# Gathered expert rows turned by moves within SBUF and VectorE blocks instead of TensorE transposes

## The chip, the cores and the metric

One core of a Trainium2 chip runs the whole program in one launch. The metric is the device time of one execution in microseconds. Five engines work beside each other, each through its own instructions in order: TensorE (PE), VectorE (DVE), ScalarE (ACT), GpSimd (POOL) and SyncE (SP, which here only issues DMAs). SBUF is the working memory with 128 partitions, PSUM holds matmul results in eight banks of 512 float32 a partition.

## The reference, cut to what matters

Attention with a window and sink tokens gives x of 1536 tokens by 512; a dense layer pair follows, `(h - tanh(h)) @ w_out` with `h = x @ w_in`. Then comes the part that the change touches, a mixture of 8 experts of which each token uses two:

```
logits = x @ w_gate + log1p(exp(x @ w_noise)) * noise
top2, top2_w = the two largest of each row, softmax of the two
for e in range(8):
    for k in range(2):
        mask = top2[:, k] == e
        h = maximum(x[mask] @ w1[e], 0)
        out[mask] += top2_w[mask, k] * (h @ w2[e])
```

## The kernel before, in words

The routing writes a table in DRAM: for each expert a list of up to 424 slots (296 for list 0, and 160 for a list 8 that holds expert 0's late tokens), each with the row of x, the row of out and the weight. Unused slots point at row 0 and write out of bounds. Tokens beyond a list's slots go to overflow sections, worked by `beyond` at the end in a loop that is entered only if there are any.

The experts run one after another, list by list. A list has eight units `u`. Unit by unit, `b_l1` makes h (128 hidden columns by 424 tokens: twelve matmuls, for the three products of split weights and split x, over four slices of 128 of the 512 inputs), `b_chain` makes hh from h (ACT the relu and upper part, DVE the remainder), and `b_l2` adds hh into four accumulators y (twelve matmuls). h has two PSUM banks, so hh of one unit must be out of its bank before the h two units later writes there. The weights come as 1 MB loads `rawi<-wm` on SP (1 KB of w1 and w2 columns a partition each) into two buffers and are split by ACT (cast) and DVE (remainder) into `wi` and `wo` some units ahead.

Around them each list v has these steps:

- `b_gather(v)` (L861): SP loads the list's table, `tab` (L866 the full tiles of 128, L868 the rest), and POOL starts one indirect gather (L857) for each tile of 128 tokens, here four, the last with 40 rows, into `graw`.
- `b_trans(v, k)` for k = 0 to 3 (L884): PE turns each tile's 128 columns of slice k (L890, `xgp<-ident,graw`), ACT casts the upper part from PSUM (L891), DVE takes the remainder (L892). The result `xg` is x of the list with inputs on partitions and tokens along the row.
- `b_prev(v)`: POOL gathers the present rows of out (`prev`).
- `b_evac`, `b_out`, `b_write`: the accumulators are copied out (`yt`, L944), PE turns them back (L972, `yp`), DVE scales and adds `prev` (L957, `y`), POOL scatters to out (L958). The gathers of `prev` wait until the scatters of the list before are in.

In the code `b_gather(e + 1)` comes in unit 1 of list e, `b_trans(e + 1, k)` in unit 4, `b_out(e - 1, m)` in units 0 to 3. The tile framework's scheduler then places every instruction in its engine's row; what an engine waits for is a semaphore, and whatever stands behind a waiting instruction of the same engine waits too.

Of the kernel before, what the change touches and what calls it, by code (L numbers as in the profile page):

```python
# [71 lines left out]
def kernel(ctx: ExitStack, tc: tile.TileContext, qkv, vsink, w64, wm, wgn, noise, out,  # L72
# [48 lines left out]
    def bank(tag, name, w=512):  # L121
        return psp.tile([P, w], F32, tag=tag, name=name, bufs=banks[tag])
# [729 lines left out]
    def tiles(v):  # L852
        w = width(v)
        return [(m, o, min(P, w - o)) for m, o in enumerate(range(0, w, P))]

    def gather(dst, src, t, m, n, rows=NT):
        nc.gpsimd.indirect_dma_start(out=dst, out_offset=None, in_=src[:rows],  # L857
                                     in_offset=bass.IndirectOffsetOnAxis(ap=t[:n, m, 0:1], axis=0),
                                     bounds_check=rows - 1, oob_is_err=False)

    def b_gather(v):  # L861
        t = gp2.tile([P, 4, 4], I32, tag="tab", name=f"tab{v}", bufs=3)
        w = width(v)
        full = w // P
        if full:
            nc.sync.dma_start(t[:, :full], table[v * W:v * W + full * P].rearrange("(m p) w -> p m w", p=P))  # L866
        if w % P:
            nc.sync.dma_start(t[:w % P, full], table[v * W + full * P:v * W + w])  # L868
        tabs[v] = t
        graw[v] = []  # L870
        for m, o, n in tiles(v):
            if m % 2 == 0:
                r = wp.tile([P, 1024], F32, tag="cacz"[m:m + 2], name=f"graw{v}_{m}", bufs=1)
            x = r[:n, (m % 2) * 512:(m % 2) * 512 + 512]
            gather(x, x2d, t, m, n, NT if v else LATE * CT)
            graw[v].append(x)

    def d_bank(name):
        spare["d"].append(spare["d"].pop(0))
        return bank(spare["d"][-1], name)  # L880
# [3 lines left out]
    def b_trans(v, k):  # L884
        w = width(v)
        if v not in xg:
            xg[v] = (yp if v % 2 else gp2).tile([P, 4, 2, W], F32R, tag="xg", name=f"xg{v}", bufs=1)
        pt = bank("as"[k % 2], f"xgp{v}_{k}") if v == 1 and k > 1 else d_bank(f"xgp{v}_{k}")
        for m, o, n in tiles(v):
            nc.tensor.transpose(pt[:, o:o + n], graw[v][m][:, k * P:(k + 1) * P], ident[:n, :n])  # L890
        nc.scalar.copy(xg[v][:, k, 0, :w], pt[:, :w])  # L891
        nc.vector.tensor_sub(xg[v][:, k, 1, :w], pt[:, :w], xg[v][:, k, 0, :w].bitcast(F32))  # L892

# [82 lines left out]
    def c_rows():  # L976
        b_gather(E)
        x = yp.tile([P, 4, WB], F32, tag="xc", name="xc", bufs=1)
        for k in range(4):
            pt = d_bank(f"xcp{k}")  # L980
            for m, o, n in tiles(E):
                nc.tensor.transpose(pt[:, o:o + n], graw[E][m][:, k * P:(k + 1) * P], ident[:n, :n])
            nc.vector.tensor_copy(x[:, k], pt[:, :WB])
        xg[E] = x

# [20 lines left out]
    def beyond(nt):  # L1006

        with ExitStack() as inner:
            op = inner.enter_context(tc.tile_pool(name="op", bufs=1, side="right"))
            tags = {}  # L1010

            def body(row, wrow):
                t = op.tile([P, 1, 4], I32, name="o_tab")
                nc.sync.dma_start(t[:, 0], table[bass.ds(row, P)])
                x = op.tile([P, 512], F32, name="o_x")
                r = op.tile([P, 512], F32, name="o_r")
                gather(x, x2d, t, 0, P)
                gather(r, out, t, 0, P)
                xt = op.tile([P, 512], F32, name="o_xt")
                tp = bank("t", "o_tp")  # L1020
                for k in range(4):
                    nc.tensor.transpose(tp[:, k * P:(k + 1) * P], x[:, k * P:(k + 1) * P], ident)
                nc.vector.tensor_copy(xt, tp)
                yb = bank("a", "o_y")
                for d in range(4):
                    w = op.tile([P, 2048], F32, name="o_w")
                    nc.sync.dma_start(w[:, None], wm[bass.ds(wrow + d, 1)].rearrange("a p n -> p a n"))
                    for s in range(2):
                        h = bank("h", "o_h")
                        for k in range(4):  # L1030
                            nc.tensor.matmul(h[:, :P], w[:, k * 256 + s * P:k * 256 + (s + 1) * P],
                                             xt[:, k * P:(k + 1) * P], start=k == 0, stop=k == 3)
                        g = op.tile([P, P], F32, name="o_g")
                        nc.vector.tensor_scalar(g, h[:, :P], 0.0, None, op0=ALU.max)
                        nc.tensor.matmul(yb, g, w[:, 1024 + s * 512:1536 + s * 512],
                                         start=d == 0 and s == 0, stop=d == 3 and s == 1)
                nc.vector.scalar_tensor_tensor(r, yb, t.bitcast(F32)[:, 0, 2:3], r, op0=ALU.mult, op1=ALU.add)
                nc.gpsimd.indirect_dma_start(out=out[:, :],
                                             out_offset=bass.IndirectOffsetOnAxis(ap=t[:, 0, 1:2], axis=0),
                                             in_=r, in_offset=None, bounds_check=NT - 1, oob_is_err=False)  # L1040

            with tc.For_i(0, E, 1) as e:
                n = nc.values_load(nt[0:1, bass.ds(e, 1)], min_val=0, max_val=OT)
                with tc.For_i(0, n, 1) as i:
                    body(e * SEC + i * P + OV, e * 4)
            n = nc.values_load(nt[0:1, E:E + 1], min_val=0, max_val=OT)
            with tc.For_i(0, n, 1) as i:
                body(i * P + (OV + E * SEC), 0)


    def in_order(k0, k1, engines):

        last = {}
        for i in nc.cur_bb.bb.instructions[k0:k1]:
            if i.engine not in engines:
                continue
            if i.engine in last:
                tc.add_manual_dep(i, last[i.engine],
                                  mybir.DependencyInfo(mybir.DependencyClass.NoSync, mybir.DependencyReason.DATA),
                                  reason="order")  # L1060
            last[i.engine] = i.name
# [146 lines left out]
    while len(routes) > 1:  # L1208
        pull_routes()
    xp_ctx.__exit__(None, None, None)  # L1210
    yp = ctx.enter_context(tc.tile_pool(name="yp", bufs=1, side="right"))
    r5 = routes.pop(0)

    def r(k=1):
# [66 lines left out]
        b_out(E, m)  # L1281
    T = mybir.EngineType
    in_order(marks["a", N1 - 1], marks["a", N1 + 8], (T.PE, T.DVE, T.Activation, T.Pool, T.SP))
    most = nc.values_load(nt[0:1, E + 1:], min_val=0, max_val=OT)
    with tc.If(most > 0):  # L1285
        beyond(nt)
# [54 lines left out]
```

## Time and profile before

| | us |
|---|---|
| three runs | 775.86, 777.5, 781.93 |
| median | 777.5 |
| the profiled execution | 779.83 |
| its span, first to last instruction | 778.1 |
| PE busy | 743.8 |
| DVE busy | 462.1 |
| ACT busy | 356.9 |
| POOL busy | 229.1 |

All times inside the profile count from the start of the span. PE ends list 0 at 452 and list 1 at 500, and then works one list every 41.4 us. "Idle before" in a row is the time in which the engine had nothing running, with what ended it. Issuing a DMA is not counted as busy; `POOL DMA_INDIRECT` rows are the issuing of gathers and scatters, not their transfer.

### The profile page before, as it was taken

What the parts mean: (1) busy time and instruction counts of PE and PEld (TensorE: products, weight loads), DVE (VectorE), ACT (ScalarE), POOL (GpSimd) and SP (SyncE); (2) the same over time, 40 slices, a digit from 0 to 9 for tenths busy, and PEclk for the clock granted to TensorE, in tenths of its full rate; (3) what the DMA queues carried; (4) which work ended last, traced back from release to release, by engine and by line L of the source; (5) the groups of instructions that cost most, each with busy time, mean ns of one, the idle gap of its engine ahead of it and who ended that gap; (6) DMA issues with size and microseconds to landing.
All of it is one profiled execution on the core that took longest, in us unless ns stands there. A gap on an engine that the chain in (4) does not pass through costs nothing. (4 is left out here: it accounts for less than half of the span.)

```text
span 778.1 us, 12237 instructions
## 1 busy us (share of the span) xinstructions
PE 743.8 (96%) x4478; PEld 666.3 (86%) x4479; DVE 462.1 (59%) x1140; ACT 356.9 (46%) x786; POOL 229.1 (29%) x240
## 2 busy tenths in 40 slices
PE   6888999999999999999989989999999999999996
PEld 3565888888999999988888969999999999999996
DVE  5899688778776684445647536455445445544221
ACT  4977688766543352334445424334333333333111
POOL 4444364521000000003064352414233342423223
PEclk9999999999999999999999979999999999999999
DMA  7453121008431140000015265534445453544331
GB/s 261 136 177 107 55 69 43 2 1 290 155 109 55 55 163 1 27 29 28 28 50 178 79 218 199 189 111 151 170 164 179 144 205 133 197 141 130 144 109 66
DMA packets 29697, 92.36 MB, mean 119 GB/s; under 512 B 8365, under 2 KB 11693, under 8 KB 22976
## 3 DMA queue, kind: packets, MB, share of 16 engines
q1 hardware_dynamic: 19232, 63.58, 24.3%
q0 software_dynamic: 8624, 23.75, 9.0%
q10 hardware_dynamic: 1776, 4.19, 1.5%
q8 instruction: 37, 0.61, 0.3%
q14 instruction: 28, 0.23, 0.1%
HBM read 78.65 MB, written 13.58 MB: 119 GB/s over the span
## 5 line engine op out<-in xcount | busy, mean ns | idle before, releaser
L907 PE MATMUL h<-xg,wi 128*128 128x424 f32 (+1 forms) x768 | 161.7, 357 | 0.0
L600 PE MATMUL h<-xT,wi 128*128 128x256 f32 x1152 | 158.6, 284 | 2.0 <-ACT wi L221 2.0
L600 PEld LDWEIGHTS h<-xT,wi 128*128 128x128 f32 x1152 | 150.8, 189 | 9.1 <-ACT wi L221 2.2
L931 PE MATMUL y<-hh,wo 128*128 128x424 f32 (+1 forms) x768 | 152.3, 347 | 0.0
L632 PE MATMUL acc<-wo,g 128*128 128x512 f32 x576 | 151.8, 396 | 0.0
L907 PEld LDWEIGHTS h<-xg,wi 128*128 128x128 f32 x768 | 138.2, 190 | 4.4
L931 PEld LDWEIGHTS y<-hh,wo 128*128 128x128 f32 x768 | 139.5, 188 | 2.5
L632 PEld LDWEIGHTS acc<-wo,g 128*128 128x128 f32 x576 | 101.4, 189 | 16.7
L917 ACT ACTIVATE hh<-h 128x424 fp32r<-128x424 f32 (+1 forms) x64 | 32.5, 510 | 152.3 <-PE h L907 131.2
L918 DVE SCALAR_TENSOR_TENSOR hh<-h,hh 128x424 fp32r<-128x424 f32 (+1 forms) x64 | 37.2, 582 | 89.6 <-ACT hh L917 72.3
L810 POOL DMA_INDIRECT table<-trow,sl x24 | 25.3, 1054 | 217.5 <-DVE sl L807 211.4
L958 POOL DMA_INDIRECT out<-y,tab x33 | 41.1, 1246 | 159.7 <-DVE y L957 159.3
L401 POOL TENSOR_TENSOR e<-e,nm 128x528 f32<-128x528 f32 (+1 forms) x48 | 50.1, 1044 | 79.1 <-DVE nm L399 47.5
L613 ACT CAST g<-th 128x256 fp32r<-128x256 f32 x96 | 38.8, 404 | 61.9 <-PE acc L632 38.6
L610 DVE TENSOR_TENSOR th<-h,th 128x256 f32<-128x256 f32 x96 | 40.4, 420 | 38.3 <-ACT th L608 32.2
L608 ACT ACTIVATE th<-h 128x256 f32<-128x256 f32 x96 | 36.6, 381 | 54.7 <-PE h L600 49.5
L615 DVE TENSOR_TENSOR g<-th,g 128x256 fp32r<-128x256 f32 x96 | 43.2, 450 | 25.2 <-ACT g L613 23.7
L390 ACT ACTIVATE e<-e,nm 128x264 f32<-128x264 f32 (+1 forms) x96 | 47.2, 492 | 23.6 <-DVE nm L377 21.4
L481 PE MATMUL xb<-pT,v 128*128 128x256 f32 x220 | 48.5, 349 | 4.5 <-DVE xT L496 2.4
L857 POOL DMA_INDIRECT prev<-out,tab x33 | 36.8, 1115 | 41.6 <-DMA out<-y,tab 21.9
L227 DVE TENSOR_TENSOR wi<-rawi,wi 128x1024 fp32r<-128x1024 f32 x32 | 39.6, 1236 | 11.5 <-ACT wi L226 8.8
L481 PEld LDWEIGHTS xb<-pT,v 128*128 128x128 f32 x220 | 33.2, 195 | 13.9 <-issue 5.4
(183 smaller groups left out, 949.2 us busy)
## 6 DMA issues: line engine op xcount, KB each, us to landing
rawi<-wm SPq DMA_DIRECT2D x31, 1024.0 KB
rawi<-w SPq DMA_DIRECT2D x8, 1024.0 KB
rawo<-w SPq DMA_DIRECT2D x8, 1024.0 KB
qr<-qkv SPq DMA_DIRECT2D x23, 256.0 KB
rawc<-wm SPq DMA_DIRECT2D x4, 1024.0 KB
out<-zero POOLq DMA_DIRECT2D x1, 3072.0 KB
x2d<-x ACTq DMA_DIRECT2D x6, 512.0 KB
v<-qkv SPq DMA_DIRECT2D x6, 256.0 KB
```

Of the source, the lines that this page charges most:

```text
L227: (nc.gpsimd if (kind, d) in POOL_SPLITS else nc.vector).tensor_sub(t[:, 1], r, t[:, 0].bitcast(F32))
L390: nc.scalar.activation(e[:, h], e[:, h], AF.Exp, bias=nm[:, h, 0:1], scale=-1.0, accum_out=nm[:, h, 2:3])
L401: nc.gpsimd.tensor_mul(e, e, nm[:, :, 3:4].to_broadcast([P, 2, C]))
L481: nc.tensor.matmul(o, l, r_, start=t == 0, stop=t == len(todo) - 1)
L600: nc.tensor.matmul(h[:, :CT], w[:, wa, k * 256 + s * P:k * 256 + (s + 1) * P], x[:, k, xa, ts], start=t == 0, stop=t == 11)
L610: nc.vector.tensor_sub(th, h[:, :CT], th)
L613: nc.scalar.copy(g[:, 0], th)
L615: nc.vector.tensor_sub(g[:, 1], th, g[:, 0].bitcast(F32))
L632: nc.tensor.matmul(acc[c][m], g[:, ga, m * P:(m + 1) * P], w[:, wa, s:s + 512], start=first and t == 0, stop=done and t == 2)
L907: nc.tensor.matmul(h[:, :width(e)], w[:, wa, k * 256 + s * P:k * 256 + (s + 1) * P], xg[e][:, k, xa, :width(e)], start=t == 0, stop=t == 11)
L931: nc.tensor.matmul(yacc[e][m][:, :width(e)], w[:, wa, s + m * P:s + (m + 1) * P], g[:, ga], start=u == 0 and t == 0, stop=u == NU2 - 1 and ...
L958: i = nc.gpsimd.indirect_dma_start(out=out[:, :], out_offset=bass.IndirectOffsetOnAxis(ap=t[:n, m, 1:2], axis=0), in_=y, in_offset=None, b ...
```

## The change

For lists 2 to 7 PE no longer turns the gathered rows. The four gathers write one tile `gr` of 128 x 4 x 512, with 128 rows in the last tile too. Sixteen DMAs on SP (a block of 32 partitions to another, each with 3 or 4 pieces of 128 floats a partition) rearrange it to `rl`: four quarter-rows of a token's 512 values, each on its own 32 partitions, in groups of 32 tokens. Then DVE's transpose turns 32x32 blocks: one instruction of 128 x 448 for each k gives `xt`, with inputs on partitions and tokens along the row. ACT's cast and DVE's remainder read `xt` from SBUF instead of `xgp` from PSUM. Since the inputs are cut in quarters of 128 and eighths of 32 in another order, w1 of experts 2 to 7 is permuted on the host, and the overflow code permutes x likewise for those experts. Lists 0, 1 and 8 keep the PE transposes, with a last tile of 128 rows. The table comes in one load. The pool `yp` is closed ahead of the overflow code, which may use its space.

```
 def b_gather(v):
     t = gp2.tile([P, 4, 4], I32, tag="tab", name=f"tab{v}", bufs=3)
     w = width(v)
-    full = w // P
-    if full:
-        nc.sync.dma_start(t[:, :full], table[v * W:v * W + full * P].rearrange("(m p) w -> p m w", p=P))
-    if w % P:
-        nc.sync.dma_start(t[:w % P, full], table[v * W + full * P:v * W + w])
+    full = (w + P - 1) // P
+    nc.sync.dma_start(t[:, :full], table[v * W:v * W + full * P].rearrange("(m p) w -> p m w", p=P))
     tabs[v] = t
+    if 2 <= v < E:
+        x = yp.tile([P, full, 512], F32, tag="gr", name=f"gr{v}", bufs=1)
+        for m, o, n in tiles(v):
+            gather(x[:, m], x2d, t, m, P)
+        r = yp.tile([P, groups(w), P], F32, tag="rl", name=f"rl{v}", bufs=1)
+        for q in range(4):
+            n = len(range(q, groups(w), 4))
+            for b in range(4):
+                nc.sync.dma_start(r[32 * b:32 * b + 32, q::4], x[32 * q:32 * q + 32, :n, P * b:P * b + P])
+        graw[v] = r
+        return
...
-        x = r[:n, (m % 2) * 512:(m % 2) * 512 + 512]
-        gather(x, x2d, t, m, n, NT if v else LATE * CT)
+        x = r[:, (m % 2) * 512:(m % 2) * 512 + 512]
+        gather(x, x2d, t, m, P, NT if v else LATE * CT)
...
 def b_trans(v, k):
...
+    if v > 1:
+        if k % 2 == 0:
+            xt = wp.tile([P, 2, 32 * groups(w)], F32, tag="cacz"[k:k + 2], name=f"xt{v}_{k}", bufs=1)
+            graw[v, k] = xt[:, 0]
+            graw[v, k + 1] = xt[:, 1]
+        pt = graw.pop((v, k))
+        nc.vector.transpose(pt.rearrange("p (g t) -> p g t", t=32), graw[v][:, :, 32 * k:32 * k + 32])
+        nc.scalar.copy(xg[v][:, k, 0, :w], pt[:, :w])
+        nc.vector.tensor_sub(xg[v][:, k, 1, :w], pt[:, :w], xg[v][:, k, 0, :w].bitcast(F32))
+        return
...
-        nc.tensor.transpose(pt[:, o:o + n], graw[v][m][:, k * P:(k + 1) * P], ident[:n, :n])
+        nc.tensor.transpose(pt[:, o:o + P], graw[v][m][:, k * P:(k + 1) * P], ident)
...
+    w1 = np.concatenate([w1[:2], w1[2:].reshape(E - 2, 4, 4, 32, 1024).swapaxes(1, 2).reshape(E - 2, 512, 1024)])
```

The scheduler places the new steps as follows. On PE the sixteen transposes of each of lists 2 to 7 are gone, and nothing else changes its order. SP, around the table of list 1 (first row) and of list 2 (the next `tab`), before:

```order
L866 DMA tab_5192<-table 128x3x4
L868 DMA tab_5192<-table 40x4
L866 DMA tab_5432<-table 128x3x4
L868 DMA tab_5432<-table 40x4
L1284 TENSOR_LOAD nt
L1284 ISA x2
L182 DMA rawi_5361<-wm 128x2048
L182 DMA rawi_5465<-wm 128x2048
```

The same place after, where `rl_5445` and `gr_5432` are list 2's:

```order
L869 DMA tab_5191<-table 128x4x4
L869 DMA tab_5430<-table 128x4x4
L1316 TENSOR_LOAD nt
L1316 ISA x2
L881 DMA rl_5445<-gr_5432 32x3x128 x2
L881 DMA rl_5445<-gr_5432 32x4x128 x2
L182 DMA rawi_5359<-wm 128x2048
L881 DMA rl_5445<-gr_5432 32x4x128 x6
L881 DMA rl_5445<-gr_5432 32x3x128 x6
L182 DMA rawi_5478<-wm 128x2048
```

The weight load that came right after the tables now stands behind four moves of list 2, and these wait for list 2's four gathers. SP around the table of list 4, before:

```order
L866 DMA tab_6145<-table 128x3x4
L868 DMA tab_6145<-table 40x4
L182 DMA rawi_6178<-wm 128x2048
L182 DMA rawi_6260<-wm 128x2048
L182 DMA rawi_6366<-wm 128x2048
L182 DMA rawi_6435<-wm 128x2048
```

After:

```order
L869 DMA tab_6145<-table 128x4x4
L182 DMA rawi_6193<-wm 128x2048
L881 DMA rl_6160<-gr_6147 32x4x128 x8
L881 DMA rl_6160<-gr_6147 32x3x128 x8
L182 DMA rawi_6275<-wm 128x2048
L182 DMA rawi_6367<-wm 128x2048
L182 DMA rawi_6436<-wm 128x2048
```

One weight load stands ahead of the sixteen moves of list 4 and three behind; lists 5 to 7 have the same order. DVE in units 1 to 3 of list 3, where list 4 is prepared, before (`y_6100` are the output tiles of list 2, `wi` and `wo` the splits):

```order
L918 SCALAR_TENSOR_TENSOR hh_6105<-h_6061,hh_6105 128x424
L957 SCALAR_TENSOR_TENSOR y_6100<-yp_0_6095,tab_5432,prev_5916 128x512
L918 SCALAR_TENSOR_TENSOR hh_6162<-h_6108,hh_6162 128x424
L227 TENSOR_TENSOR wi_6368<-rawi_6260,wi_6368 128x1024
L957 SCALAR_TENSOR_TENSOR y_6100<-yp_1_6136,tab_5432,prev_5916 128x512
L227 TENSOR_TENSOR wo_6335<-rawi_6178,wo_6335 128x1024
L918 SCALAR_TENSOR_TENSOR hh_6204<-h_6165,hh_6204 128x424
```

After:

```order
L942 SCALAR_TENSOR_TENSOR hh_6105<-h_6061,hh_6105 128x424
L981 SCALAR_TENSOR_TENSOR y_6100<-yp_0_6095,tab_5430,prev_5930 128x512
L942 SCALAR_TENSOR_TENSOR hh_6177<-h_6108,hh_6177 128x424
L908 STREAM_TRANSPOSE xt_0_6306<-rl_6160 128x448 x2
L981 SCALAR_TENSOR_TENSOR y_6100<-yp_1_6136,tab_5430,prev_5930 128x512
L908 STREAM_TRANSPOSE xt_2_6313<-rl_6160 128x448
L910 TENSOR_TENSOR xg_6305<-xt_0_6306,xg_6305 128x424 x2
L910 TENSOR_TENSOR xg_6305<-xt_2_6313,xg_6305 128x424
L908 STREAM_TRANSPOSE xt_2_6313<-rl_6160 128x448
L227 TENSOR_TENSOR wo_6336<-rawi_6193,wo_6336 128x1024
L942 SCALAR_TENSOR_TENSOR hh_6219<-h_6180,hh_6219 128x424
```

The four block transposes and three of the remainders now stand between the hh of two neighbouring units in the list's second and third unit; before, the remainders stood in its fifth and sixth, behind PE's transposes, and a weight split stood here in their place.

## Rows read from the trace of the kernel before

**Rows 1.** The page: busy time, and the granted clock in 40 slices.

```profile
PE 743.8 (96%) x4478; PEld 666.3 (86%) x4479; DVE 462.1 (59%) x1140; ACT 356.9 (46%) x786; POOL 229.1 (29%) x240
...
PEclk9999999999999999999999979999999999999999
```

**Rows 2.** Stretches: busy us (instructions) of each engine, granted clock, DMA share, GB/s.

```profile
453.00:457.40 4.40, 0.60 (x2) 0.22 (x2) 0.92 (x2) 0.41 (x1) 2.28 (x3) 0.77 0.90 289
457.40:466.00 8.60, 8.59 (x29) 6.89 (x30) 2.40 (x4) 2.26 (x5) 4.01 (x4) 0.52 0.56 201
...
541.00:582.40 41.40, 41.40 (x226) 39.38 (x226) 20.76 (x27) 15.01 (x22) 14.38 (x12) 1.00 0.49 165
```

**Rows 3.** PE in order of time, list 4's turn: start, length, what.

```profile
575.01 1.33 PE L890 MATMUL xgp<-ident,graw 128*128 128x128 f32 x8
...
582.39 2.48 PE L907 MATMUL h<-xg,wi 128*128 128x424 f32 x12
...
586.99 1.31 PE L907 MATMUL h<-xg,wi 128*128 128x424 f32 x6
```

**Rows 4.** Groups by shape, 430 to 778 us: busy us, mean ns, idle before.

```profile
L890 PE MATMUL xgp<-ident,graw 128*128 128x128 f32 x84 | 15.7, 295 | 0.3 <-DMA graw<-x2d,tab 0.3
...
L890 PE MATMUL xgp<-ident,graw 40*128 40x40 f32 x28 | 7.4, 263 | 3.5 <-DMA graw<-x2d,tab 3.5
```

**Rows 5.** PE in order of time at the turn of list 1.

```profile
453.59 0.33 PE L890 MATMUL xgp<-ident,graw 128*128 128x128 f32 x1 [0.32 <-DMA graw<-x2d,tab]
457.41 3.59 PE L890 MATMUL xgp<-ident,graw 40*128 40x40 f32 x13 [3.50 <-DMA graw<-x2d,tab]
```

**Rows 6.** POOL in order of time, gathers of list 1 and after.

```profile
446.37 1.06 POOL L857 DMA_INDIRECT graw<-x2d,tab  x1 [3.39 <-DMA tab<-table]
...
450.77 1.20 POOL L857 DMA_INDIRECT graw<-x2d,tab  x1 [0.30 <-issue]
...
454.90 0.99 POOL L857 DMA_INDIRECT prev<-out,tab  x1 [0.30 <-issue]
```

**Rows 7.** SP's queue in order of time: tables of list 1, weight loads.

```profile
443.86 0.38 SPq L866 DMA_DIRECT2D tab<-table  x1
444.29 0.41 SPq L868 DMA_DIRECT2D tab<-table  x1
...
451.13 0.34 SPq L182 DMA_DIRECT2D rawi<-wm  x1
...
552.73 0.33 SPq L182 DMA_DIRECT2D rawi<-wm  x1
```

**Rows 8.** POOL in order of time: last scatter to list 4's gathers.

```profile
530.21 1.65 POOL L958 DMA_INDIRECT out<-y,tab  x1 [4.09 <-DVE y L957]
...
542.76 1.66 POOL L857 DMA_INDIRECT graw<-x2d,tab  x1 [0.30 <-issue]
...
547.33 0.98 POOL L857 DMA_INDIRECT graw<-x2d,tab  x1 [0.30 <-issue]
```

**Rows 9.** Stretches, columns as in rows 2, around the end of list 4's gathers.

```profile
547.40:550.10 2.70, 2.70 (x16) 2.65 (x15) 1.43 (x3) 1.99 (x4) 0.92 (x1) 1.00 0.84 334
550.10:552.70 2.60, 2.60 (x15) 2.54 (x14) 2.60 (x3) 1.35 (x2) 0.00 (x0) 1.00 0.02 6
```

**Rows 10.** DVE in order of time, units 2 to 4 of list 3.

```profile
558.31 0.60 DVE L918 SCALAR_TENSOR_TENSOR hh<-h,hh 128x424 fp32r<-128x424 f32 x1 [2.13 <-ACT hh L917]
559.25 1.23 DVE L227 TENSOR_TENSOR wi<-rawi,wi 128x1024 fp32r<-128x1024 f32 x1 [0.34 <-ACT wi L226]
...
570.57 0.75 DVE L957 SCALAR_TENSOR_TENSOR y<-yp,tab,prev 40x512 f32<-40x512 f32 x1
```

**Rows 11.** PE in order of time: three h's, the first and the last.

```profile
560.19 2.57 PE L907 MATMUL h<-xg,wi 128*128 128x424 f32 x12
...
570.28 1.41 PE L907 MATMUL h<-xg,wi 128*128 128x424 f32 x6
```

**Rows 12.** ACT in order of time: the split that follows in list 1.

```profile
471.06 1.04 ACT L226 CAST wi<-rawi 128x1024 fp32r<-128x1024 f32 x1
```

More of the change, by code (lines that the diff above doesn't have):

```diff
@@ L859, in gather, with groups @@
                                      bounds_check=rows - 1, oob_is_err=False)
+    def groups(w):
+        return (w + 31) // 32
     def b_gather(v):
@@ L981, in c_rows @@
             for m, o, n in tiles(E):
-                nc.tensor.transpose(pt[:, o:o + n], graw[E][m][:, k * P:(k + 1) * P], ident[:n, :n])
+                nc.tensor.transpose(pt[:, o:o + P], graw[E][m][:, k * P:(k + 1) * P], ident)
             nc.vector.tensor_copy(x[:, k], pt[:, :WB])
@@ L1010, in beyond, with body @@
             tags = {}
-            def body(row, wrow):
+            def body(row, wrow, turned=False):
                 t = op.tile([P, 1, 4], I32, name="o_tab")
@@ L1019, in body @@
                 xt = op.tile([P, 512], F32, name="o_xt")
+                if turned:
+                    nc.vector.tensor_copy(xt.rearrange("p (k q j) -> p k q j", k=4, q=4),
+                                          x.rearrange("p (q k j) -> p k q j", k=4, q=4))
+                    x = xt
+                    xt = op.tile([P, 512], F32, name="o_xp")
                 tp = bank("t", "o_tp")
@@ L1040, in body @@
                                              in_=r, in_offset=None, bounds_check=NT - 1, oob_is_err=False)
[L1042 to L1045, printed above, removed]
+            for e0, e1 in ((0, 2), (2, E)):
+                with tc.For_i(e0, e1, 1) as e:
+                    n = nc.values_load(nt[0:1, bass.ds(e, 1)], min_val=0, max_val=OT)
+                    with tc.For_i(0, n, 1) as i:
+                        body(e * SEC + i * P + OV, e * 4, e0 > 0)
             n = nc.values_load(nt[0:1, E:E + 1], min_val=0, max_val=OT)
@@ L1210 @@
     xp_ctx.__exit__(None, None, None)
-    yp = ctx.enter_context(tc.tile_pool(name="yp", bufs=1, side="right"))
+    yp_ctx = tc.tile_pool(name="yp", bufs=1, side="right")
+    yp = yp_ctx.__enter__()
     r5 = routes.pop(0)
@@ L1283 @@
     in_order(marks["a", N1 - 1], marks["a", N1 + 8], (T.PE, T.DVE, T.Activation, T.Pool, T.SP))
+    yp_ctx.__exit__(None, None, None)
     most = nc.values_load(nt[0:1, E + 1:], min_val=0, max_val=OT)
```

## The prediction, made before the changed kernel was run

> **What bounds the kernel now.** I read the page first, then the table of stretches for the expert stage, then PE's order of time, then the engines and queues that feed it. The page has PE busy for 743.8 of 778.1 us, with the granted clock down in few slices [rows 1]. The table of stretches says it more sharply: in 541 to 582.4 us, which is one whole list (call it a round of 41.4 us), PE is busy for 41.40 of 41.40 us at full clock, while DVE works 20.76, ACT 15.01, and the DMA engines are used to 0.49 [rows 2]. So in the lists a microsecond of PE is a microsecond of the kernel, and everything else counts only when it makes PE wait. One stretch is different: from 453 to 457.4 us PE does 0.60 us of work while the DMA engines are 0.90 busy, and the 8.6 us after it run at a clock of 0.52, the lower of the two levels [rows 2].
>
> **The transposes that leave PE.** The turn of a list begins on PE at 575.01 and holds sixteen transposes, one unit of twelve h matmuls cut in three, and twelve y matmuls; the next h begins at 582.39. An undisturbed pair of h and y takes 586.99 - 582.39 = 4.60 us [rows 3]. The turn therefore costs 7.38 - 4.60 = 2.78 us. Six lists lose it (of 124 such transposes 96 go): 6 x 2.78 = **-16.7 us**, all on the engine that has no gap.
>
> **Full last tiles.** Lists 0, 1 and 8 keep the transposes on PE, with 128 rows instead of 40 or 32 in the last tile: 12 transposes that go from 263 to 295 ns mean [rows 4], 12 x 0.03 = **+0.4 us** (0 from below, as a shape of one length; 12 x 0.3 = 3.5 from above, if each were a whole transpose more).
>
> **List 1.** PE waits 3.50 us there, until 457.41, for the fourth gather of the list [rows 5]. POOL had issued it at 450.77 and was done with it at 451.97 [rows 6], but SP issued a 1 MB load at 451.13 [rows 7], and the engines then were 0.90 busy. In the changed order this load stands behind the first four moves of list 2, and these wait for list 2's gathers, which POOL cannot begin before its last prev gather is out, at 454.90 + 0.99 = 455.9 [rows 6]. So the fourth gather meets an idle DMA. What that is worth I read from list 4: its fourth gather is issued by 547.33 + 0.98 = 548.3 [rows 8], and the DMA engines fall from 0.84 to 0.02 at 550.1 [rows 9], 1.8 us later. That gives 451.97 + 1.8 = 453.8; 88 more rows at 2.70 us for 424 [rows 9] add 0.6. PE would go on at 454.4: -3.0 us. If the clock then does not fall, 8.6 us at 0.52 become 4.5: another -4.1 us, together -7. Against this stands the load that went back in the queue: four gathers take 547.33 + 0.98 - 542.76, about 5.6 us [rows 8], so they are out at 461.5 and landed at 463.3; four moves take 1.7 us more, and the load leaves at 465 instead of 451. With the 6.3 us that it took before (451.13 to 457.4, when the busy stretch of rows 2 ends) it lands at 471.3. Before, ACT split it at 471.06 [rows 12]. On the old times it is just in time; with PE 7 us earlier it is late, and ACT, which has h's activation behind the split, waits. I give back 3 of the 7 and take **-4 us** (bounds -7, all kept; +3, if the wait outlasts the gain).
>
> **The new chain for lists 2 to 7.** Per list come 16 moves on SP, four DVE transposes of 448 wide, and the split now reads SBUF. Neither the moves nor the block transpose are in this trace. A move: back-to-back issues on SP stand 0.43 us apart [rows 7], and POOL could use the tables at 446.37, 1.7 us after the second issue ended at 444.70 [rows 6, 7]. So 16 x 0.43 + 1.7 = 8.6 us from gather to last landing (from below 16 x 0.34 + 1.7 = 7.1, by the load's own issue time in rows 7; from above 16 x 0.43 + 6.3 = 13.2, if the last one queues behind a 1 MB load). I take 8.6, since the two tables are the nearest kind of transfer. A block transpose: the longest DVE row works 1024 elements in 1.23 us [rows 10], so 448 take 0.54; from above 1.23 whole, from below 0.3 (twice that rate). I take 0.55, because all DVE rows near it are about this dear per element. The split's subtraction I leave at the 0.60 of a 424-wide row [rows 10] (0.5 to 0.7).
>
> The Trainium skill (VectorE: DVE Perf Modes, The three transpose paths and Rules for kernel authors) speaks against the swap: for a 128x128 transpose it says to use TensorE where PSUM will do, and it gives DVE 311 ns for such a block in bf16, so an estimate by that page is 3.5 x 311 = 1.09 us here, with which each round below is 2.2 us longer and the whole about 768. No run here shows that price yet.
>
> DVE takes its work in order, so the transposes hold up what stands behind. In the round of list 4 (times of before, less the 2.78 us of the turn that lies between the last out scatter and here): the hh row ahead of the transposes ends at 558.31 + 0.60 - 2.78 = 556.1 [rows 10]. The gathers are in at 550.1 [rows 9], the moves at 558.7. DVE waits 2.6 us. Behind the transposes come 4 x 0.55 + 0.75 (y) + 3 x 0.60 + 1.22 (split) = 6.0 us until the next hh, which ends at 565.3. That hh frees one of two h banks: the h begun at 560.19 has its bank written again at 570.28 [rows 11], less 2.78 is 567.5. So 2.2 us are left, and PE does not wait. But the chain closes on itself: the last y of the list follows at 565.3 + 0.75 + 0.60 + 1.23 + 0.60 + 0.75 = 569.2 instead of 570.57 + 0.75 - 2.78 = 568.5 [rows 10], and from it hang the out scatter, prev, the next gathers and the next moves: from 530.21 [rows 8] to 558.7 are 28.5 us, plus 10.5 to the last y and 0.3 to its scatter, 39.3 us around. PE's new round is 41.4 - 2.8 = 38.6. Each round falls 0.7 us further back, and the 2.2 us last for about lists 4 to 7. I take **+1 us** (0 to +18; the upper end is below). The weights' loads, which SP now issues behind the moves, are 5 us late (552.73 before [rows 7], about 557.4 in the same times); a split that waits for one comes after the transposes anyway.
>
> **Sum.** -16.7 + 0.4 - 4 + 1 = -19.3. The profiled execution took 779.83 us (778.1 of span and 1.7 around it): 760.5. It is 2.3 above the median of the three runs, 777.5, from which the same sum gives 758.2. I forecast 759.5.
>
> **Rivals.**
> *The chain takes PE's place.* If a move waits behind a load (stage 13.2 us), list 4 loses 4.6 - 2.2 = 2.4 us, and the three rounds after it are 43.9 instead of 38.6, 3 x 5.3 = 15.9: together 18, and 760.5 - 1 + 18 = 778, no change. With block transposes of 1.23 us it is 2.7 more per round: 0.5 + 3 x 3.4 = 10.7, 770. Half way 772. For it speaks that 39.3 stands so near to 38.6; against it that the DMA engines are idle right after the gathers [rows 9].
> *Slower: the moves run one after another.* Each of 16 small transfers then costs up to the 1.7 us from issue to use. With s us from gather to last move, list 4 loses s - 10.8 and each of three further rounds s - 7.9. The gain of 19.3 is used up, and 1% more, when 4s - 34.5 = 27, s = 15.4, that is 0.86 us a move. At 1.0, between 0.43 and 1.7, s is 17.7, the loss 36, and the time 797. For it speaks only that nothing in this trace moves SBUF to SBUF. Against it: SP issued two table loads 0.43 apart and both were usable 1.7 us after the second [rows 6, 7].
> The Trainium skill (SBUF — State Buffer, Summary: rules for kernel authors) is on this rival's side: for a transfer bound by DMA it wants 128 partitions and "one DMA, not several", and here are sixteen on 32 partitions. The trace neither agrees nor disagrees: it has no such set.
> *List 1 alone.* Nothing gained there is 764, all of it 757.5; both lie in the forecast's own range, 751 to 768. That the transposes stay on PE is no rival: the changed order has none for lists 2 to 7.
>
> **How the numbers follow.** Forecast with its own range 0.67; chain in PE's place 0.20; slower 0.13. A measurement of this kernel tells 1% from no change, here 769.7 and 785.3. All of the first case is faster; of the second 0.06 ends under 769.7 and 0.14 over it; the third is slower: 0.73, 0.14, 0.13. The range has to reach the second case, to 779, and from below 751 (all of list 1 kept, no give-back, the median's basis, and some room): about 0.13 above and 0.04 below are left out.
>
> **What would show it.** Right: no transposes in PE's rows for lists 2 to 7; rounds near 38.6 to 39.5 us with PE without a gap; the fourth gather of list 1 in by 455; DVE idle two to three microseconds ahead of the first block transpose of lists 4 to 7; block transposes of 0.5 to 0.6 us; the last move landed under 9 us after the gathers. Wrong: PE gaps ahead of h, with hh late behind a block transpose; block transposes over 1 us; moves further apart than 0.5 us; a clock below 1.00 anywhere in lists 2 to 7; or rounds that stay at 41.4.

## The result and the profile after

The changed kernel takes **789.7 us** (median of 5 runs, 784.9 to 792.1) against 778.3 for the kernel before in the same comparison: a ratio of 1.014, 95% interval 1.009 to 1.019. It is slower by 1.4%; the forecast was 759.5, with a range from 751 to 779. The profiled execution took 784.91 us, 783.2 of them span. Ratios and intervals here are of fast runs alone, and of e11's four runs one was slow (782.5 us), so that its time below is the median of the other three.

The page after, busy time and the granted clock in 40 slices (before: [rows 1]):

```profile
PE 733.0 (94%) x4382; PEld 659.6 (84%) x4383; DVE 468.3 (60%) x1164; ACT 354.8 (45%) x786; POOL 227.4 (29%) x240
...
PEclk9999999999999999999999999989989998999998
```

PE has 96 matmuls fewer and 10.8 us less to do, yet the span is 5.1 us longer. The clock row shows where to look: its one dip of before, at list 1, is gone, and there are three new ones further on in the lists (the fourth 8 is the end of the program, behind the lists). The table of stretches after (columns as in [rows 2]), one list of 40 us and the three dips:

```profile
530.00:570.00 40.00, 37.49 (x198) 35.56 (x197) 14.24 (x19) 11.41 (x17) 13.19 (x10) 1.00 0.50 151
...
514.70:521.50 6.80, 5.58 (x16) 5.29 (x17) 6.34 (x11) 3.11 (x5) 1.12 (x1) 0.50 0.84 340
...
572.70:579.50 6.80, 4.80 (x14) 4.50 (x15) 5.40 (x8) 2.10 (x5) 2.01 (x2) 0.50 0.59 206
...
658.00:664.90 6.90, 5.70 (x16) 5.35 (x17) 4.85 (x8) 2.27 (x5) 2.01 (x2) 0.51 0.54 186
```

Before, PE was busy 41.40 of 41.40 us in such a stretch [rows 2]. Now it has gaps, and after a gap it ran at the lower of the two levels (0.50, 1.2 GHz) for some 6.8 us. Twelve matmuls of h took 4.61 us there and 2.57 at full clock, so the 5.58 + 4.80 + 5.70 = 16.1 us of work done at that level would have taken 9.0: some 7 us are the clock's.

PE after, in order of time, at list 1 and in the round in which list 4 is made ready:

```profile
453.19 1.64 PE L914 MATMUL xgp<-ident,graw 128*128 128x128 f32 x13 [0.31 <-DMA graw<-x2d,tab]
454.59 0.87 PE L931 MATMUL h<-xg,wi 128*128 128x424 f32 x3
...
570.47 0.62 PE L996 MATMUL yp<-ident,yt 128*40 128x128 f32 x4 [2.58 <-DVE y L981]
574.70 4.61 PE L931 MATMUL h<-xg,wi 128*128 128x424 f32 x12 [3.61 <-DVE hh L942]
```

List 1 went as forecast, or better: the fourth gather makes PE wait 0.31 us instead of 3.50 [rows 5], the clock stays up. Later PE waits for y and then for hh, and the next h takes 4.61 us instead of the 2.57 of [rows 11]. The waits after, from 430 us on (what waited for what: us in total, times, longest):

```profile
ACT wi L226 <- DMA rawi<-wm: 63.7, 23, 6.7
ACT xg L909 <- DVE xt L908: 50.0, 14, 12.3
DVE xt L908 <- DMA rl<-gr: 47.5, 6, 12.2
PE h L931 <- DVE hh L942: 13.8, 6, 5.6
...
PE yp L996 <- DVE y L981: 3.6, 2, 2.6
...
SPq L881 <- DMA gr<-x2d,tab: 62.9, 9, 14.3
```

PE's 13.8 + 3.6 us and 0.4 of issue, together 18, and the clock's 7 are the loss of the lists in this trace. Three waits can stand behind them: DVE's for the moves, with ACT's for DVE's transposes behind it; ACT's for weight loads (2.8 us in all in the kernel before); and SP's, at the head of the moves, for the gathers. SP, DVE, ACT and POOL after, in that same round, in order of time:

```profile
543.57 0.33 SPq L182 DMA_DIRECT2D rawi<-wm  x1
556.69 10.23 SPq L881 DMA_DIRECT2D rl<-gr  x16
567.37 7.16 SPq L182 DMA_DIRECT2D rawi<-wm  x2
```

```profile
556.10 0.60 DVE L942 SCALAR_TENSOR_TENSOR hh<-h,hh 128x424 fp32r<-128x424 f32 x1 [1.82 <-ACT hh L941]
568.61 1.17 DVE L908 STREAM_TRANSPOSE xt<-rl 128x448 f32<-128x448 f32 x2 [11.91 <-DMA rl<-gr]
...
574.05 0.59 DVE L942 SCALAR_TENSOR_TENSOR hh<-h,hh 128x424 fp32r<-128x424 f32 x1
```

```profile
569.29 1.07 ACT L909 CAST xg<-xt 128x424 fp32r<-128x424 f32 x2 [10.41 <-DVE xt L908]
...
572.21 1.04 ACT L226 CAST wi<-rawi 128x1024 fp32r<-128x1024 f32 x1 [0.67 <-DMA rawi<-wm]
573.16 0.52 ACT L941 ACTIVATE hh<-h 128x424 fp32r<-128x424 f32 x1
```

```profile
534.38 1.64 POOL L982 DMA_INDIRECT out<-y,tab  x1 [5.94 <-DVE y L981]
...
547.57 1.03 POOL L857 DMA_INDIRECT gr<-x2d,tab  x1 [0.30 <-issue]
```

SP starts no weight load between 543.57 and 567.37; before there was one at 552.73 [rows 7]. DVE stands 11.91 us ahead of the first block transpose, 18 us pass between two hh. And the gathers themselves come late (547.57, where before the first was at 542.76 [rows 8]), because the last scatter of the list ahead came at 534.38: the circle is closed.

What holds hh is read from the rows just ahead of it. ACT stands 10.41 us for the transposes, and only then 0.67 for the load; and what PE waits for at 570.47 is a y that DVE computes right behind its first transposes. At the first and longest gap, 5.59 us ahead of 515.92, where list 3 is made ready, no load comes in at all: hh follows the first block transpose on DVE, and ACT had done its part of it by 503.1.

```profile
514.74 0.65 DVE L908 STREAM_TRANSPOSE xt<-rl 128x448 f32<-128x448 f32 x1 [12.17 <-DMA rl<-gr]
515.31 0.56 DVE L942 SCALAR_TENSOR_TENSOR hh<-h,hh 128x424 fp32r<-128x424 f32 x1
```

DVE's six waits are 1.1, 12.2, 11.9, 5.8, 10.4 and 6.2 us for lists 2 to 7, and PE's three long gaps ahead of h fall on the three above 10. But when ACT then comes to its next split, the load is 0.4 to 0.7 us short of landed in all three, so this trace alone can't say what either wait would cost without the other. The block transposes are nearly as cheap as forecast, 0.63 us (group by line, 430 us to the end):

```profile
L908 DVE STREAM_TRANSPOSE xt<-rl 128x448 f32<-128x448 f32 x24 | 14.6, 629 | 47.5 <-DMA rl<-gr 47.5
```

### The profile page after: what moved, and what is told of

Its sections match the earlier page's. It is cut to its first block, busy times and chain, and to the rows that moved or that the text cites. A ratio compares the mean times of both kernels' runs of the same rounds, so it can differ in the third digit from the quotient of the medians.

```text
span 783.2 us, 12207 instructions
## 1 busy us (share of the span) xinstructions
PE 733.0 (94%) x4382; PEld 659.6 (84%) x4383; DVE 468.3 (60%) x1164; ACT 354.8 (45%) x786; POOL 227.4 (29%) x240
## 4 chain that ended last, share of the span: by engine, by line
PE 41%; issue 25%; DMA 10%; POOL 8%; DVE 8%; SPq 3%; ACT 3%; POOLq 0%; DVEq 0%; ACTq 0%
PE h L600 16%; PE acc L632 15%; PE xb L481 4%; DMA out<-y,tab 3%; PE s L366 3%; POOL out L982 3%; SPq L881 2%; DMA prev<-out,tab 2%; POOL gr L857 2%; DMA rawi<-wm 2%; PE pt L448 2%; POOL prev L857 2%; DVE e L377 1%; DMA tab<-table 1%; DMA gr<-x2d,tab 1%
## 5 line engine op out<-in xcount | busy, mean ns | idle before, releaser
L931 PE MATMUL h<-xg,wi 128*128 128x424 f32 (+1 forms) x768 | 162.1, 361 | 13.9 <-DVE hh L942 13.8
L931 PEld LDWEIGHTS h<-xg,wi 128*128 128x128 f32 x768 | 142.0, 194 | 20.0 <-DVE hh L942 15.5
L955 PE MATMUL y<-hh,wo 128*128 128x424 f32 (+1 forms) x768 | 154.3, 350 | 0.4 <-issue 0.4
L982 POOL DMA_INDIRECT out<-y,tab x33 | 37.7, 1141 | 173.9 <-DVE y L981 167.3
L227 DVE TENSOR_TENSOR wi<-rawi,wi 128x1024 fp32r<-128x1024 f32 x32 | 41.2, 1286 | 50.3 <-ACT wi L226 40.9
L226 ACT CAST wi<-rawi 128x1024 fp32r<-128x1024 f32 x32 | 33.5, 1048 | 64.5 <-DMA rawi<-wm 64.4
```

Of the source, the lines that this page charges most:

```text
L227: (nc.gpsimd if (kind, d) in POOL_SPLITS else nc.vector).tensor_sub(t[:, 1], r, t[:, 0].bitcast(F32))
L931: nc.tensor.matmul(h[:, :width(e)], w[:, wa, k * 256 + s * P:k * 256 + (s + 1) * P], xg[e][:, k, xa, :width(e)], start=t == 0, stop=t == 11)
L955: nc.tensor.matmul(yacc[e][m][:, :width(e)], w[:, wa, s + m * P:s + (m + 1) * P], g[:, ga], start=u == 0 and t == 0, stop=u == NU2 - 1 and ...
L982: i = nc.gpsimd.indirect_dma_start(out=out[:, :], out_offset=bass.IndirectOffsetOnAxis(ap=t[:n, m, 1:2], axis=0), in_=y, in_offset=None, b ...
```

## The experiments

Three theories. **A**: DVE waits in its row for the moves, ACT for DVE's transposes, and hh stands behind. **B**: SP waits at the moves for the gathers, and weight loads stand behind. **C**: the moves' packets, or the transposes themselves, cost the time. In the edits, `after(i_, 1)` puts an instruction behind the one written last for the same engine, without a semaphore. All ratios are to the kernel before, timed beside the run.

### e1_pin: DVE's order alone

```diff
-            nc.vector.transpose(pt.rearrange("p (g t) -> p g t", t=32), graw[v][:, :, 32 * k:32 * k + 32])
+            i_ = nc.vector.transpose(pt.rearrange("p (g t) -> p g t", t=32), graw[v][:, :, 32 * k:32 * k + 32])
+            after(i_, 1)
```

> The changed kernel with its block transposes kept on VectorE where the program writes them (unit 4 of a list) instead of some two units earlier; the 16 moves and SP's order are untouched. Theory A (VectorE waits in order for the moves, about 12 us a list, and hh stands behind): PE's waits for hh fall from 13.8 us to under 5, the granted clock no longer falls in the lists (8 us), about 767 us. Theory B (SP is blocked by the moves, so the weight loads, the splits, the last y, the next gathers are late): ACT still waits some 60 us for weights, the last y is as late as before, 780 to 790. Theory C (the moves' packets crowd the other transfers, or the block transposes themselves are too dear): 785.

Measured 794.9 us, ratio 1.026 (1.021 to 1.031). The waits of e1_pin:

```profile
SPq L881 <- DMA gr<-x2d,tab: 66.3, 10, 14.2
...
ACT wi L226 <- DMA rawi<-wm: 75.6, 21, 10.7
DVE xt L908 <- DMA rl<-gr: 41.9, 4, 12.3
...
PE h L932 <- DVE hh L943: 20.3, 9, 4.7
```

B's numbers came, and more. But the edit hardly moved DVE's wait (41.9 us for 47.5): the first transpose still stands behind the first of a list's four y, and the moves land no earlier. So this run says nothing against A.

### e2_load_first: SP's order

The moves become a function `b_moves` of their own, called in unit 4 and pinned in the order written, so that on SP two weight loads stand between the table and the moves instead of one:

```diff
                 b_gather(e + 1)
+            if u == 4 and e:
+                b_moves(e + 1)
```

> The changed kernel with the 16 moves of a list written in unit 4 instead of unit 1, held on SP behind the weight load that they now hold up; the block transposes follow them as the scheduler likes. Theory A: VectorE waits as long as before, since the moves land no earlier, 785 to 792. Theory B: ACT's wait for weights falls from 63.7 us to under 15, the last y of a list and with it the next gathers come 4 to 5 us earlier, about 770. Theory C: 785.

Measured **759.9 us**, ratio 0.981 (0.976 to 0.987). SP and the waits of e2_load_first:

```profile
533.65 9.13 SPq L182 DMA_DIRECT2D rawi<-wm  x2
543.00 11.79 SPq L891 DMA_DIRECT2D rl<-gr  x16
554.90 0.53 SPq L182 DMA_DIRECT2D rawi<-wm  x1
```

```profile
ACT wi L226 <- DMA rawi<-wm: 22.4, 16, 3.3
...
DVE xt L919 <- DMA rl<-gr: 0.9, 1, 0.9
...
SPq L891 <- DMA gr<-x2d,tab: 1.0, 1, 1.0
```

The same 16 moves, now 11.8 us long, cost nothing: the loads are out before them, the gathers are in when SP gets there, and DVE's wait is gone too (47.5 to 0.9 us). The one edit changed two rows: the scheduler put the first transpose behind the third y of a list (558.35 us, the last move having been issued by 554.79) instead of the first. So e2 takes away what A blames as well as what B blames. In lists 2 to 7 PE has no gap. ACT's wait for weights was to fall under 15 and fell to 22.4, which nobody waits for. Only list 1 lost again what it had gained (a wait of 4.40 us for the fourth gather), because the load that the moves had held back now leaves early.

### e4_wide: a fourth of the DMAs, the same bytes

```diff
-                for b in range(4):
-                    nc.sync.dma_start(r[32 * b:32 * b + 32, q::4], x[32 * q:32 * q + 32, :n, P * b:P * b + P])
+                nc.sync.dma_start(r[:, q::4], x[:, :n, P * q:P * q + P])
```

> The changed kernel with 4 moves of 128 partitions in place of 16 of 32: the same bytes in the same 512-byte pieces, a fourth of the DMAs. It leaves out the sorting of a list's rows into 32-token groups, so lists 2 to 7 compute on rows in another order. If SP pays by the DMA (0.64 us each), the moves are issued in 2.6 us instead of 10.3 and both A and B give up 7.7 us of wait a list: about 765. If SP pays by the piece, a move takes about 2.4 us and nothing changes: 785. Theory C, since bytes and pieces are the same: 785.

Measured 799.2 us, ratio 1.027 (1.023 to 1.031): outside every expectation. SP and the waits of e4_wide:

```profile
561.46 2.69 SPq L880 DMA_DIRECT2D rl<-gr  x4
```

```profile
SPq L880 <- DMA gr<-x2d,tab: 72.0, 10, 15.8
...
PE h L930 <- DVE hh L941: 29.2, 6, 11.0
```

SP pays by the DMA, as the first case had it (2.69 / 4 = 0.67 us, against 10.23 / 16 = 0.64, with four times the bytes each), but the 7.7 us a list that this saves are worth nothing, since the waits are no shorter: SP stands 72.0 us for gathers and DVE 54.8 for moves, and its places in the rows are others again. The longest gap, 11.0 us, is in list 1: there DVE stands 12.7 us for the moves of list 2 and ACT 11.6 for the transposes, and the split behind them (472.84) waits for no load. That is A's wait without B's.

### e8_sp_wait_alone, e8_wait4, e12_sp_wait_late: the wait put into the kernel before

The kernel before keeps its transposes on PE. Behind a list's gathers it gets 16 tiny DMAs on SP (4 in e8_wait4) that read the gathered rows. In both no load stands between the table and them, where the changed kernel has one, so the place is a little worse than that of the moves:

```diff
+        if 2 <= v < E:
+            d = yp.tile([P, 64], F32, tag="dm", name=f"dm{v}", bufs=1)
+            for m in range(16):
+                i_ = nc.sync.dma_start(d[:40, 4 * m:4 * m + 4], graw[v][m % 4][:40, :4])
+                after(i_, 1)
```

> The kernel before, with the transposes on PE and VectorE as it was, and 16 tiny DMAs a list on SP (40 partitions of 16 bytes from the gathered rows to a scratch tile that nobody reads), written where the change writes its moves, and so waiting there for the gathers. Theory B (SP's order alone makes the stalls): weight loads 10 us late, ACT's wait for weights from 2.8 us to over 40, PE waits for hh, 785 to 800. Rival (it also takes VectorE's wait for the moves): PE keeps its pace, 775 to 780.

> As e8_sp_wait_alone, the kernel before with tiny DMAs on SP behind each list's gathers, but 4 instead of 16 a list. If the time is lost by waiting for the gathers and not by issuing (13.65 us for 16 there, so some 3.4 here): 805 to 819. If it goes with their number: 785 to 792.

> e8_sp_wait_alone with its 16 tiny DMAs a list written in unit 4, so that on SP two weight loads stand between the table and them instead of none. If what costs is which loads stand behind the wait for the gathers: SP finds the gathers landed, ACT's wait for weights falls from 113 us to under 25, PE keeps its pace, 775 to 783. If 16 DMAs a list on SP cost by their issue time wherever they stand: 790 or more.

Measured 818.6, ratio 1.055 (1.051 to 1.059); 808.3, ratio 1.036 (1.034 to 1.039); and 784.3, ratio 1.009 (1.005 to 1.012). The waits of e8_sp_wait_alone, and a row of ACT's order of time:

```profile
SPq L882 <- DMA graw<-x2d,tab: 69.2, 18, 14.8
...
ACT wi L226 <- DMA rawi<-wm: 113.4, 21, 16.3
...
PE h L914 <- DVE hh L925: 25.7, 5, 6.8
...
570.10 1.04 ACT L226 CAST wi<-rawi 128x1024 fp32r<-128x1024 f32 x1 [16.30 <-DMA rawi<-wm]
```

So B's mechanism is enough without moves and without a wait of DVE: DMAs of 640 bytes that nobody reads, in that place, cost 41 us, 5.5%. ACT waits 16.3 us for weights, and hh stands behind the split on ACT and on DVE. With 4 DMAs it is still 29 us, so most of it is the wait and not the count (PE waits 20.0 us there for ACT's copies of y, which stand behind the split). At the late place the 16 cost 7.6 us, between the two expectations: the place takes 34 of the 41 us, and 16 issues of 12.43 / 16 = 0.78 us are not free even there (ACT waits 40.8 us for weights, PE has small gaps).

### e10_dve_no_wait and e11_sp_no_wait: DVE's wait taken away, then both

In e10 the transposes read `ident`, in e11 the moves do:

```diff
-            nc.vector.transpose(pt.rearrange("p (g t) -> p g t", t=32), graw[v][:, :, 32 * k:32 * k + 32])
+            nc.vector.transpose(pt.rearrange("p (g t) -> p g t", t=32), ident[:, None, 32 * k:32 * k + 32].to_broadcast([P, groups(w), 32]))
```

```diff
-                    nc.sync.dma_start(r[32 * b:32 * b + 32, q::4], x[32 * q:32 * q + 32, :n, P * b:P * b + P])
+                    nc.sync.dma_start(r[32 * b:32 * b + 32, q::4], ident[32 * q:32 * q + 32, None].to_broadcast([32, n, P]))
```

> The changed kernel with its 16 moves a list in place on SP, but the block transposes read a constant tile and wait for no move. It leaves out the use of the gathered rows of lists 2 to 7. If VectorE's wait for the moves is what stalls PE (theory A): 757 to 768. If SP's wait for the gathers, in front of the weight loads, does it by itself (theory B, as in e8_sp_wait_alone, where VectorE had no such wait and the kernel lost 41 us): ACT's wait for weights stays over 50 us and the time is 785 to 805.

> The changed kernel with the 16 moves a list on SP reading a constant tile, so that SP waits for no gather and VectorE for nothing late; number, shape and bytes of the moves stay. It leaves out the use of the gathered rows of lists 2 to 7. If the price is the wait at the head of the moves (theory B): 752 to 765. If it is their issue time (96 x 0.60 us on SP) or their packets among the other transfers (theory C): 775 to 785.

Measured 805.6, ratio 1.033 (1.030 to 1.036), and 770.3, ratio 0.987 (0.983 to 0.990). The waits of e10_dve_no_wait, and a row of ACT's order of time where list 3 is made ready:

```profile
SPq L881 <- DMA gr<-x2d,tab: 79.9, 12, 15.7
...
ACT wi L226 <- DMA rawi<-wm: 130.3, 21, 15.4
...
PE h L931 <- DVE hh L942: 30.5, 5, 7.1
...
520.19 1.04 ACT L226 CAST wi<-rawi 128x1024 fp32r<-128x1024 f32 x1 [13.69 <-DMA rawi<-wm]
```

With no wait of DVE for a move the kernel is not faster but slower, so A's wait isn't needed for the loss. Where list 3 is made ready, SP has the order of the changed kernel (table, one load, 16 moves, loads), and there PE's gap only comes one unit later and is hardly shorter, 4.20 us for 5.59: ACT stands for the load instead of the transposes. From list 4 on the scheduler put the moves right behind the table, ahead of one more weight load, which makes B's part dearer than in the changed kernel. e11, where neither SP nor DVE has anything late to wait for, is fast again. It missed its range by 5 us, and not by the lists: the scheduler started moves and loads early, and list 1's fourth gather was late again (3.07 us of PE's time, and a clock of 0.87 in the mean of 452 to 490 us). From 490 to 730 us PE is busy 237.1 of 240, against 209.5 in e10's same stretch. Issue time and packets of 96 moves, theory C, cost at most that little.

### e9_pool_moves: another queue

```diff
-                    nc.sync.dma_start(r[32 * b:32 * b + 32, q::4], x[32 * q:32 * q + 32, :n, P * b:P * b + P])
+                    nc.gpsimd.dma_start(r[32 * b:32 * b + 32, q::4], x[32 * q:32 * q + 32, :n, P * b:P * b + P])
```

> The changed kernel with the 16 moves issued by POOL, right behind the gathers, instead of by SP, which then only loads tables and weights. Theory B: ACT's wait for weights is back under 10 us and PE has no wait for hh in lists 2 to 7: 755 to 765, unless a move costs POOL over 1 us, when scatters and gathers queue behind 16 of them: then 770 to 790. Theory A: VectorE waits as long as in the changed kernel, 785.

Measured 824.0 us, ratio 1.060 (1.056 to 1.065), far outside. The waits of e9_pool_moves, and DVE's order of time where list 4 is made ready:

```profile
ACT xg L909 <- DVE xt L908: 92.0, 10, 19.1
...
DVE xt L908 <- DMA rl<-gr: 74.3, 6, 16.4
...
PE h L931 <- DVE hh L942: 39.8, 5, 9.8
...
572.50 1.70 DVE L908 STREAM_TRANSPOSE xt<-rl 128x448 f32<-128x448 f32 x3 [16.42 <-DMA rl<-gr]
574.18 0.60 DVE L942 SCALAR_TENSOR_TENSOR hh<-h,hh 128x424 fp32r<-128x424 f32 x1
```

A move costs POOL 0.56 us, well under 1. SP now only loads, so B's wait isn't there, and yet PE stands 39.8 us for hh, three times as long as in the changed kernel. In each of the five gaps hh comes right behind block transposes that waited 10.0 to 16.4 us for the moves, and ACT's next split finds its weights there (574.93 in the round shown). So A's wait is enough too. Theory A had expected DVE to wait as long as in the changed kernel; it waited longer, 74.3 us for 47.5. The moves land no earlier by the other queue: the first transposes start 16.7 us after POOL is done with the last gather, 16.4 in the changed kernel. POOL's own wait for the gathers (26.3 us) holds up its scatters (one whose y was ready at 556.08 leaves at 572.98), but the last of a list, on which the next gathers hang, comes at 587.66 after 4.91 us for DVE's y, not for POOL.

### e5_list1, e6_first_list1 and e3_late_pinned: list 1, and the best version

e5 is the kernel before with one load sent from ACT's queue; e6 is e2 with the same edit; e3 is e2 with the block transposes pinned in unit 5.

```diff
-            q.dma_start(t, wm[d - 8])
+            if d == 15:
+                i_ = nc.scalar.dma_start(t, wm[d - 8])
+                after(i_, 1)
+            else:
+                q.dma_start(t, wm[d - 8])
```

> The kernel before with one edit: the weight load that ran beside list 1's fourth gather (issued at 451.13 us on SP) is issued from ACT's queue behind list 1's casts. My theory of list 1 (that load is what made the fourth gather late by 3 us and, through the idle PE, the clock fall for 8.6 us): PE's 3.50 us wait falls under 1 us, no fall of the clock at 455 us, 770.5 us against 777.5. Rival (the gather is late for another reason, or the later load makes a split late by as much): 775 to 779.

> e2_load_first (moves written in unit 4, behind a weight load: 759.9 us) with e5_list1's edit (the load beside list 1's fourth gather goes to ACT's queue: 6 us off the kernel before). If the two are independent: list 1's wait of 4.40 us goes from e2's trace and no clock falls near 455 us, 753 to 754. If the later load makes list 1's splits late, because SP's moves of list 2 come soon after: 757 to 762.

> e2_load_first with the block transposes written in unit 5 and kept there on VectorE. If VectorE's order matters by itself (theory A in what is left of it): other waits than e2's, below 757 or, if list e+1's first h then waits for xg, above 764. If only SP's order mattered (theory B): as e2, 758 to 762.

Measured 770.5, ratio 0.993 (0.990 to 0.995); **755.4**, ratio 0.973 (0.970 to 0.977); and 764.6, ratio 0.985 (0.980 to 0.990). PE at list 1 in e5, then one list of e6 in the table of stretches:

```profile
450.99 2.23 PE L894 MATMUL xgp<-ident,graw 40*128 40x40 f32 x13 [0.17 <-DMA graw<-x2d,tab]
```

```profile
537.60:576.20 38.60, 38.60 (x209) 37.51 (x208) 21.88 (x30) 14.99 (x22) 14.68 (x12) 1.00 0.62 202
```

The load beside list 1's gather costs the kernel before 5.8 us, and the two gains add up (16.4 of e2 and 5.8, against 21.9): e6 beats both kernels, 21.9 us under the one before, though its 755.4 lies between its two expectations. A list takes 38.6 us instead of 41.4 with PE busy throughout. e3 is no better than e2; its 764.6 is in the branch in which the next list's first h waits for xg, and PE does wait 1.1 us for it. With the intervals of e2 and e3 overlapping, all that is shown is that this later place of the transposes gains nothing more.

### e13_one_loop, e14_free_later, e16_before_share: the end of the program

One part of the loss is not in the lists. From the end of the last scatter (774.12 + 0.91 = 775.03 us) to the end of the span the kernel before has 3.1 us, the changed one 783.2 - 777.34 = 5.9, e6 5.9 too.

```diff
-            for e0, e1 in ((0, 2), (2, E)):
+            for e0, e1 in ((0, E),):
```

```diff
-    yp_ctx.__exit__(None, None, None)
     most = nc.values_load(nt[0:1, E + 1:], min_val=0, max_val=OT)
+    yp_ctx.__exit__(None, None, None)
```

The first is e13, the second e14, both on e6; e16 closes the pool `yp` ahead of that read in the kernel before.

> e6_first_list1 with one loop over the experts' overflow instead of two (the loop isn't entered with these inputs; entered, it would compute lists 2 to 7 on unturned rows). From the end of the last scatter to the end of the span the kernel before takes 3.1 us and the changed one 5.9. If the second loop's code makes the 2.8 us: 3.1 here. If the shared space does: 5.9.

> e6_first_list1 with the lists' pool given back behind the read of the overflow count instead of ahead of it. If the engines' wait for that pool ahead of the read makes the 2.8 us at the end: 3.1 to 4 us from the last scatter to the end of the span; else 5.9.

> The kernel before with the one edit that the overflow pool takes the lists' pool's space, given back ahead of the read of the overflow count. If the sharing by itself makes the 2.8 us: 5.9 us from the last scatter to the end of the span; if the second loop does: 3.1.

The ends measured 3.4, 5.9 and 3.1 us, from one profile each: the second overflow loop, which is never entered, costs some 2.5 us at the end, the sharing of space nothing. (Their times, 761.4, 765.7 and 780.5, are single runs. e13 and e14 lost list 1's gain again, with ACT's casts of xg starting 1.4 us apart behind a releaser that the profile doesn't place; why, is open.)

## Why the prediction was wrong

**The transposes that leave PE: right.** e6 against e5 is the swap alone, in a place where it harms nothing: 770.5 - 755.4 = 15.1 us. The prediction's terms for it are -16.7 + 0.4 + 1 = -15.3. The round of 38.6 us is the predicted one. Hidden in this is the 2.8 us of the end, a term that the prediction didn't have; the lists gave 2.6 us more than the sum.

**List 1: right mechanism, too cautious.** -4 was taken, with -7 as the bound. The first h of list 1 came 6.3 us earlier (454.59 against 460.93), and e5 gives 5.8 for the same thing alone.

**The chain: the step that failed.** The prediction had DVE wait 2.6 us for the moves in the round of list 4, saw 2.2 us of room behind that and concluded "and PE does not wait": +1 us. The forecast of where DVE would stand was right (its hh ends at 556.7, forecast 556.1). But the moves let the first transpose start at 568.6 and not at 558.7, and DVE waited 11.9 us, ACT 10.4 behind it. Two sizes make up these 10 us. The gathers were in at 556.69, when SP issued the first move, instead of 550.1, since they had been issued 4.8 us later than before and landed 4 us after the last of them. And from there to the first transpose it took 11.9 us instead of 8.6 (moves 0.64 us apart for 0.43); the second alone is 4 x 11.9 - 34.5 = 13 us by the prediction's own formula for a longer stage. Besides, only list 4 was gone through. For list 3 the scheduler put the first transpose further ahead, soon after the copies `yt` of the last list, when the gathers had just landed (DVE there at 502.57, SP's first move at 502.96): 12.2 us of wait and the first 5.6 us of PE's time, before anything had gone round a circle.

A second line of the same part went wrong with it: the weight loads behind the moves are "5 us late", and "a split that waits for one comes after the transposes anyway". The prediction counted how long 16 issues take and not how long SP stands at the first of them. SP comes to the moves before the gathers have been issued (after 543.57 us; gathers from 547.57, first move 556.69) and then issues for 10 us. The load was 14.6 us late (567.37 against 552.73). In the changed kernel the split does come after the transposes, as the prediction said, and waits only 0.67 us more; but that is because the transposes were as late. e8 and e10 show that the late loads stop PE without them.

So two rows stood too early in front of data that wasn't there: DVE, with ACT behind it, in front of the moves, and SP in front of the gathers. Either is enough (e9 and list 1 of e4; e8 and e10), and in the changed kernel, where the load lands within 0.7 us of when the other wait lets ACT at it, each stands in for the other. The price of both is after against e6: 789.7 - 755.4 = 34 us, where the sum had 1. How much each would cost alone in the changed kernel no run shows, since e2 and e6 take both away.

The runs by their two waits (430 to 760 us):

| run | SP waits for gathers, us | DVE waits for moves, us | ratio to before |
|---|---|---|---|
| e6, e2, e3 | 1.5, 1.0, 6.6 | none, 0.9, 4.7 | 0.973, 0.981, 0.985 |
| e11 | none | none | 0.987 |
| e12 (transposes on PE) | 2.9 | - | 1.009 |
| the changed kernel, e1, e4 | 62.9, 66.3, 72.0 | 47.5, 41.9, 54.8 | 1.014, 1.026, 1.027 |
| e10 | 79.9 | none | 1.033 |
| e8_wait4, e8 (transposes on PE) | 59.4, 69.2 | - | 1.036, 1.055 |
| e9 (moves on POOL) | none | 74.3 | 1.060 |

The total of ACT's waits for weights doesn't sort them: it is 63.7 us in the changed kernel and 68.3 in e11, which is fast.

**The block transposes: right.** 0.63 us for 0.55. The 1.09 us estimated from the Trainium skill (VectorE: DVE Perf Modes, The three transpose paths) was too dear. The Trainium skill's rule to use TensorE for a 128x128 transpose where PSUM will do (VectorE: DVE Perf Modes, Rules for kernel authors) isn't borne out here. In the lists PE bounds the kernel, and giving the work to DVE is worth 15 us (e6 against e5).

**The rivals.** "The chain takes PE's place" had the right shape, a circle from gather to gather longer than PE's round, and the right wait, DVE's. Its price of at most 18 us was too low, it left SP's wait out, and it needed a move behind a load or dear transposes, which were not what happened. "The moves run one after another" fell on the right side for a wrong reason: at 0.64 us they stay under its 0.86, and e4, with 4 moves, is as slow. The Trainium skill (SBUF — State Buffer, Summary: rules for kernel authors) stood beside that rival with its one DMA in place of several. The runs agree as far as the issue goes (2.69 us for 4 moves of 128 partitions, 10.23 for 16 of 32), but e4 gained no time by it.

Of the signs named for a wrong forecast, three were there: PE gaps ahead of h, with hh late behind a block transpose; moves over 0.5 us apart; a clock under 1.00 in the lists.

## What to carry to other kernels

An instruction that waits for its data holds up everything behind it in its row, on a queue of DMAs (SP in e8) as on an engine (DVE and ACT in e9). When a stage is added, go through the row of every engine that takes part, for every round: ask when its source is there, when the row gets to it, and what stands behind it, and only then what it costs to do. Put it behind the work that is needed sooner, in the order of when each can start. Such a wait shows as one row of the waits (SP for the gathers, DVE for the moves), far from where the time is lost (PE for hh); and where two of them end together, taking one away changes little.

## What the runs showed of the hardware that was not expected

Back to back on SP, DMAs came 0.64 (the changed kernel) to 0.74 us (e2) apart for 32 partitions of 3 or 4 pieces of 512 bytes, 0.67 for 128 partitions of the same (e4), and 0.78 to 0.85 for 40 partitions of 16 bytes (e12, e8): the time does not go with the bytes. On POOL a move took 0.56 us (e9). A loop that is not entered cost some 2.5 us at the end of the program (e13 against e6, one profile each).
